# A decode step on one core: ScalarE sums 48 of a tile's 256 positions, and the maxima move into the next multiplication

## The chip, the cores and the metric

The kernel runs on one core of one Trainium2 chip. The metric is the device time of one launch in microseconds, taken over several runs. One of the runs was recorded by the hardware profiler; every time below that belongs to an instruction comes from that execution, counted from its span's start.

## The reference, cut to what matters

Two sequences of one new token each (B = 2, D = 512) go through attention over a cache of 8192 positions with 32 heads of 128, and then through a gated layer. All tensors are bfloat16.

```python
h  = x + attention(layernorm(x), k_cache, v_cache, wq, wo)
h2 = h + mlp(layernorm(h), W_gate, W_up, W_down)

# attention, Sq = 1, 32 heads, Dh = 128, Sk = 8192
q      = x @ wq                                   # (2, 32, 1, 128)
scores = einsum("bhqd,bhkd->bhqk", q, k) * Dh ** -0.5
o      = einsum("bhqk,bhkd->bhqd", softmax(scores), v)
out    = o.reshape(2, 1, 4096) @ wo
# mlp: ((x @ W_gate) * (gate > 0) * (x @ W_up)) @ W_down, F = 1376
```

The two caches hold 268 MB together, the weights some 12.6 MB. Each element of the cache is used once.

## The kernel before, in words

**Tiles and steps.** There are 16 steps: for each of the two sequences, eight groups of four heads. A step works on a K tile and a V tile of 8.4 MB each: 128 partitions, 32 to a head, with 256 positions of 128 values in each partition. The tiles pass through three buffers, `buf[0..2]`. `k_at` and `v_at` say which: V(i) goes into the buffer of K(i) once K(i) has been used up (except V(0) and V(15)), and K(i+1) into the buffer of V(i-2). All loads are issued on the SP queue, in the order K(i+1), V(i), and each waits for its buffer to be free. The projection weights `wq` and the row of queries `qrow` lie in `buf[1]` at the start, where V(0) goes; the output and MLP weights go into the buffer of K(15) at the end.

**Scores of step i** (`scores(i)`). VectorE multiplies the whole K tile in place by the query, spread over the partitions in `qrep` (line 344). Then it halves the 128 values of a position by additions, 128 to 64 to 32 to 16 to 8 (line 373), and a reduction sums the last eight into a column of `scol` (line 377). The last `NACT[i]` positions are left out of this tree: ScalarE sums each by a copy with `accum_out` (line 362), 8 positions in most steps, 24 and 32 in the first two, 16 in the last. Then VectorE takes the maximum of `scol` in each partition (`pm`, line 385), and TensorE spreads it with the softmax scale (`mx_ps`, line 387).

**The step before, in between.** After the multiplication of step i come `collect(i-2)` (ScalarE copies the finished products out of PSUM, line 434), `powers(i-1)` (VectorE reduces `mx_ps` to the negated maximum `nm`, line 303; ScalarE computes the exponentials into `pgz` in four instructions, line 306), `turn(i-2)` (TensorE turns collected products into columns) and `values(i-1)` (TensorE multiplies V(i-1) by the powers, 64 products in a loop, line 422; for the last two steps 256 small products, line 408). The order of the instructions on TensorE, VectorE, ScalarE and the SP queue is the order of the program.

**The ends.** Before step 0 the queries are made in eight groups (`make_q`): four products into `q_ps`, a copy by ScalarE into `qrow`, eight small products that spread them into `r_ps`, and a copy into `qrep`. In step 15, 48 of the positions are not multiplied by VectorE: TensorE transposes them eight at a time (line 326), ScalarE copies the transposed block into `kT` (line 331), and TensorE multiplies it by the query (line 335). After step 15 come the weights' loads (lines 464 to 482), `powers(15)`, `values(15)`, the output projection (line 516) and the MLP (lines 552 to 598).

Of the kernel before, what the change touches and what calls it, by code (L numbers as in the profile page):

```python
# [7 lines left out]
ACT = mybir.ActivationFunctionType  # L8
# [15 lines left out]
def kernel(  # L24
# [13 lines left out]
    nc = tc.nc  # L38
# [14 lines left out]
    TPC = 8  # L53
    NPE = 48
    T4 = 4
# [56 lines left out]

    qrep = consts.tile([P, B, NG, Dh], bf16)
    pgz = consts.tile([P, NT * H4], bf16)
# [54 lines left out]
    with tc.manual_schedule(engines=ORDERED):  # L169
# [62 lines left out]


        def make_q(n):
            q_ps = ps2.tile([P, 512], f32, tag="tp")
# [5 lines left out]
            nc.scalar.activation(out=qrow[0:B, n * 512:(n + 1) * 512], in_=q_ps[0:B, :], func=ACT.Copy)  # L241
            r_ps = ps2.tile([P, B, Dh], f32, tag="tp", name="r_ps")
# [52 lines left out]


        mx = {}

        def powers(i):
            b, g = steps[i]  # L300
            mx_ps, scol = mx.pop(i)
            nm = small.tile([P, H4], f32, tag="nm")
            nc.vector.tensor_reduce(out=nm, in_=mx_ps, axis=AXIS.X, op=ALU.min)  # L303
            for j in range(H4):
# [6 lines left out]
        def scores(i):  # L311
            b, g = steps[i]
            kt = buf[k_at[i]]
            npe = NPE if i == N - 1 else 0
            nmul = NT - npe
            nv = nmul - NACT[i]
            scol = small.tile([P, NT], f32, tag="scol")

            if npe:
                sc_ps = ps.tile([P, NPE, H4], f32, tag="sc")  # L320

                def transposed(c0):
                    t_ps = ps2.tile([P, TPC, P], bf16, tag="tp", name="t_ps")
                    for k in range(TPC):
                        t = nmul + c0 + k
                        nc.tensor.transpose(t_ps[:, k, :], kt[:, t * Dh:(t + 1) * Dh], ident)  # L326
                    return t_ps

                t_ps = transposed(0)
                for c0 in range(0, NPE, TPC):  # L330
                    nc.scalar.activation(out=kT, in_=t_ps.rearrange("p t s -> p (t s)"), func=ACT.Copy)  # L331
                    if c0 + TPC < NPE:
                        t_ps = transposed(c0 + TPC)
                    for t in range(TPC):
                        nc.tensor.matmul(  # L335
                            out=sc_ps[:, c0 + t, :], lhsT=kT[:, t * P:(t + 1) * P], rhs=_free(qT, b, [[B, H4]]),
                            start=True, stop=True,
                        )

            pieces = 4 if i == 0 else 1  # L340
            for t0 in range(0, NT, NT // pieces):
                n = min(NT // pieces, nmul - t0)
                kv = _free(kt, t0 * Dh, [[Dh, n], [1, Dh]])
                nc.vector.tensor_tensor(  # L344
                    out=kv, in0=kv, in1=_free(qrep, (b * NG + g) * Dh, [[0, n], [1, Dh]]), op=ALU.mult,
                )

            if i >= 2:
                collect(i - 2)
            if i >= 1:  # L350
                powers(i - 1)
            if i >= 2:
                turn(i - 2)
            left = waiting[:]
            if i >= 1:
                values(i - 1)
                tc.no_sync_barrier()
                if i + 1 < N:
                    load_k(i + 1)
            for t in range(nv, nmul):  # L360
                whole = small.tile([P, Dh], f32, tag="whole")
                nc.scalar.activation(  # L362
                    out=whole, in_=kt[:, t * Dh:(t + 1) * Dh], func=ACT.Copy, accum_out=scol[:, t:t + 1],
                )
            if npe:
                for j in range(H4):
                    r = slice(j * QP, (j + 1) * QP)
                    nc.scalar.activation(out=scol[r, nmul:NT], in_=sc_ps[r, :, j], func=ACT.Copy)
            width = Dh
            while width > 8:  # L370
                half = width // 2
                lo = _free(kt, 0, [[Dh, nv], [1, half]])
                nc.vector.tensor_tensor(  # L373
                    out=lo, in0=lo, in1=_free(kt, half, [[Dh, nv], [1, half]]), op=ALU.add,
                )
                width = half
            nc.vector.tensor_reduce(  # L377
                out=scol[:, 0:nv], in_=_free(kt, 0, [[Dh, nv], [1, 8]]), axis=AXIS.X, op=ALU.add,
            )

            for e in left:
                waiting.remove(e)
                normalise(e)
# [3 lines left out]
            nc.tensor.matmul(  # L387
                out=mx_ps.rearrange("p a b -> p (a b)"), lhsT=_free(pm, 0, [[0, P]]), rhs=nscale,
                start=True, stop=True,
            )  # L390
            mx[i] = mx_ps, scol

# [89 lines left out]
        nc.sync.dma_start(out=wd_r[0:LASTW], in_=_dram(B_W_down, FULL * P * D, [[D, LASTW], [1, D]]))  # L482

        turn(N - 2)
        powers(N - 1)
# [142 lines left out]
```

## Time and profile before

| | us |
|---|---|
| runs (3) | 675.11, 675.25, 677.73; median 675.25 |
| profiled execution, its own time | 676.83 |
| its span | 675.0 |
| PE busy | 365.0 (54%) |
| VectorE (DVE) busy | 573.7 (85%) |
| ScalarE (ACT) busy | 151.9 (23%) |
| bytes moved | 281.29 MB, mean 417 GB/s over the span |

How to read it: PE is TensorE, DVE is VectorE, ACT is ScalarE, SP the queue that issues the loads. A row of a timeline has start, duration, engine, line, operation, what it writes and reads, and in brackets how long its engine had been idle and for what it waited. A row of the groups has a count, the busy time, the mean of one in nanoseconds, and the idle time before. A row of the windows has the stretch, its length, the busy time of each engine, TensorE's granted clock, the DMA engines' busy share and the rate in GB/s.

### The profile page before, as it was taken

The numbers are of one execution on the slowest core, as the hardware profiler recorded it, in microseconds if no ns is written. First come the engines' busy times: TensorE is split into PE (matmuls) and PEld (weight loads), VectorE is DVE, ScalarE is ACT, GpSimd is POOL, SyncE is SP. The second block draws the span as 40 slices with busy tenths as digits, with TensorE's granted clock in tenths as the row PEclk, the third lists the DMA queues.
The fourth block names the chain that finished last, engine by engine and source line by source line (L and its number), as shares of the span: only waits on it lengthen the run. The fifth ranks groups of instructions, "written<-read, shape, count | busy, mean of one in ns | idle before, by whom it ended". The sixth has DMA issues, their size and how long they took to land. (4 is left out here: it accounts for less than half of the span.)

```text
span 675.0 us, 7725 instructions
## 1 busy us (share of the span) xinstructions
PE 365.0 (54%) x1963; PEld 126.5 (19%) x1963; DVE 573.7 (85%) x164; ACT 151.9 (23%) x525; POOL 8.5 (1%) x52
## 2 busy tenths in 40 slices
PE   2710373736647373663727466274745737277666
PEld 1100011111111121111102111011211111012556
DVE  0899989699897989979797997989899797998801
ACT  2360634003030401303030030303103040221820
POOL 5000000000000000000000000000000000000000
PEclk9999997987959698796969869598896959789555
DMA  9999999999999999999999999999999999999996
GB/s 371 438 433 435 435 373 435 435 435 435 377 436 435 435 427 435 435 377 431 431 432 419 396 435 416 435 400 435 424 416 435 396 435 404 431 416 412 417 417 255
DMA packets 6918, 281.29 MB, mean 417 GB/s; under 512 B 786, under 2 KB 884, under 8 KB 1524
## 3 DMA queue, kind: packets, MB, share of 16 engines
q1 hardware_dynamic: 6896, 281.06, 98.0%
q8 instruction: 10, 0.16, 0.1%
q14 instruction: 8, 0.07, 0.0%
q10 hardware_dynamic: 4, 0.00, 0.0%
HBM read 281.05 MB, written 0.00 MB: 416 GB/s over the span
## 5 line engine op out<-in xcount | busy, mean ns | idle before, releaser
L422 PE MATMUL po<-buf,pgz 128*16 x868 | 288.9, 410 | 90.0 <-issue 88.3
L344 DVE TENSOR_TENSOR buf<-buf,qrep 128x32768 bf16<-128x32768 bf16 (+2 forms) x19 | 272.9, 14362 | 52.4 <-DMA buf<-in_A_k_cache_dram 52.4
L373 DVE TENSOR_TENSOR buf<-buf 128x15872 bf16<-128x15872 bf16 (+7 forms) x64 | 252.0, 3937 | 1.7
L422 PEld LDWEIGHTS po<-buf,pgz 128*16 x868 | 78.8, 91 | 305.6 <-issue 264.2
L396 PE MATMUL po<-buf,pgz 128*16 128x512 bf16 x28 | 14.3, 614 | 158.5 <-ACT whole L362 158.5
L434 ACT ACTIVATE ob<-po 16x512 f32<-16x512 f32 x14 | 8.2, 585 | 325.0 <-PEq L416 324.9
L306 ACT ACTIVATE pgz<-scol,nm 32x256 bf16<-32x256 f32 x64 | 55.1, 862 | 111.0 <-DVE nm L303 106.2
L362 ACT ACTIVATE whole<-buf 128x128 f32<-128x128 bf16 x176 | 54.4, 309 | 6.0 <-DVE buf L344 0.5
L377 DVE TENSOR_REDUCE scol<-buf 128x248 f32<-128x1984 bf16 (+3 forms) x16 | 34.7, 2170 | 1.6
L362 ACT ACTIVATION_READ_ACCUMULATOR whole<-buf 128x1 f32 x176 | 32.8, 186 | 0.0
L396 PEld LDWEIGHTS po<-buf,pgz 128*16 128x16 bf16 x28 | 1.4, 90 | 160.9 <-issue 160.9
L387 PE MATMUL mx_ps<-nscale,pm 128*128 128x128 f32 x32 | 8.0, 334 | 24.9 <-DVE pm L385 19.8
L237 PE MATMUL q_ps<-buf,xn 128*2 128x512 bf16 x32 | 14.9, 621 | 2.9 <-DMA buf<-in_A_wq_dram 2.9
L408 PE MATMUL o_ps<-pgz,buf 128*128 128x4 bf16 x512 | 14.2, 166 | 3.4 <-issue 3.4
L306 ACT ACTIVATION_READ_ACCUMULATOR pgz<-scol,nm 32x1 f32 x64 | 16.0, 250 | 0.0
L293 DVE RECIPROCAL rz<-o_ps 128x4 f32<-128x4 f32 (+2 forms) x4 | 1.0, 253 | 17.3 <-PE o_ps L408 17.3
L408 PEld LDWEIGHTS <-buf 128*128 128x128 bf16 x512 | 14.3, 105 | 3.5 <-issue 3.5
L331 ACT ACTIVATE kT<-t_ps 128x1024 bf16<-128x1024 bf16 x6 | 6.1, 1023 | 28.9 <-PE t_ps L326 26.4
L387 PEld LDWEIGHTS mx_ps<-nscale,pm 128*128 128x128 f32 x32 | 5.2, 202 | 29.1 <-issue 18.9
L385 DVE TENSOR_REDUCE pm<-scol 128x1 f32<-128x256 f32 x16 | 6.7, 418 | 2.1 <-ACT whole L362 0.8
L218 DVE COPY xc<-x_ps 128x8 f32<-128x8 f32 x1 | 0.2, 166 | 8.5 <-PE x_ps L214 8.5
L241 ACT ACTIVATE buf<-q_ps 2x512 bf16<-2x512 f32 x8 | 4.7, 586 | 11.2 <-PE q_ps L237 11.2
(89 smaller groups left out, 85.9 us busy)
## 6 DMA issues: line engine op xcount, KB each, us to landing
buf<-in_A_k_cache_dram SPq DMA_DIRECT2D x4, 2048.0 KB, 23.7
buf<-in_A_v_cache_dram SPq DMA_DIRECT2D x2, 4096.0 KB, 24.8
buf<-in_A_wq_dram SPq DMA_DIRECT2D x1, 4096.0 KB, 12.6
buf<-in_A_wo_dram SPq DMA_DIRECT2D x1, 2048.0 KB, 17.3
buf<-in_A_wo_dram SPq DMA_DIRECT2D x2, 1024.0 KB, 20.2
buf<-in_B_W_gate_dram SPq DMA_DIRECT2D x1, 1376.0 KB
buf<-in_B_W_up_dram SPq DMA_DIRECT2D x1, 1376.0 KB, 25.8
buf<-in_B_W_down_dram SPq DMA_DIRECT2D x1, 768.0 KB, 26.9
```

The source lines that it names most:

```text
L237: nc.tensor.matmul(out=q_ps[0:B, :], lhsT=xn[:, c, :], rhs=wq_sb[:, c, n * 512:(n + 1) * 512], start=(c == 0), stop=(c == KC - 1),)
L306: nc.scalar.activation(out=_free(pgz[r, :], j, [[H4, NT]]), in_=scol[r, :], func=ACT.Exp, scale=SCALE, bias=nm[r, j:j + 1], accum_out=zc[r ...
L344: nc.vector.tensor_tensor(out=kv, in0=kv, in1=_free(qrep, (b * NG + g) * Dh, [[0, n], [1, Dh]]), op=ALU.mult,)
L362: nc.scalar.activation(out=whole, in_=kt[:, t * Dh:(t + 1) * Dh], func=ACT.Copy, accum_out=scol[:, t:t + 1],)
L373: nc.vector.tensor_tensor(out=lo, in0=lo, in1=_free(kt, half, [[Dh, nv], [1, half]]), op=ALU.add,)
L377: nc.vector.tensor_reduce(out=scol[:, 0:nv], in_=_free(kt, 0, [[Dh, nv], [1, 8]]), axis=AXIS.X, op=ALU.add,)
L385: nc.vector.tensor_reduce(out=pm, in_=scol, axis=AXIS.X, op=ALU.max)
L387: nc.tensor.matmul(out=mx_ps.rearrange("p a b -> p (a b)"), lhsT=_free(pm, 0, [[0, P]]), rhs=nscale, start=True, stop=True,)
L396: nc.tensor.matmul(out=made[i][0:H4 * T4, :], lhsT=pgz[:, u * H4 * T4:(u + 1) * H4 * T4], rhs=v[:, u * T4 * Dh:(u + 1) * T4 * Dh], start=( ...
L408: nc.tensor.matmul(out=o_of(i)[:, 0, H4 * g:H4 * (g + 1)], lhsT=v[:, t * Dh:(t + 1) * Dh], rhs=pgz[:, H4 * t:H4 * (t + 1)], start=(t == 0) ...
L422: nc.tensor.matmul(out=made[i][0:H4 * T4, :], lhsT=pgz[:, bass.ds((w * LOOP + u) * (H4 * T4), H4 * T4)], rhs=v[:, bass.ds((w * LOOP + u) * ...
L434: nc.scalar.activation(out=ob[32 * k:32 * k + H4 * T4, :], in_=made.pop(i)[0:H4 * T4, :], func=ACT.Copy,)
```

## The change

- `NACT` becomes 48 for most steps, 64 for step 1 and 32 for step 15. These are now the first positions of the tile, not the last.
- The multiplication is in three parts: the positions that ScalarE sums, then 144 (`MIDDLE`), then the rest. In step 0 it stays in four pieces.
- The maximum of step i-1 and its product on TensorE move out of step i-1 into step i, between the first and the second part (`best(i - 1)`). `powers(i-1)` comes after the second part. `scol` now has two buffers.
- ScalarE sums 16 positions (`FIRST`) before `collect` and `powers`, the others after `values`. Its full-width output, which nobody reads, goes to PSUM (`whole` from pool `ps`, tag `acc`) instead of SBUF.
- The projections run one group ahead: `make_q(n)` now comes before `spread_q(n - 1)`. `qrep` becomes one tile for each sequence, so the copy into it is two instructions; `kT` uses the room of the first one.
- Step 15: 32 positions instead of 48 go through TensorE; their first two blocks are transposed after the second part of the multiplication, the copies into `kT` come after `powers(14)`, and `values(14)` after them. The maximum of step 15 is taken after the weights' loads in the program.

```diff
-    NPE = 48
+    NPE = 32
+    FIRST = 16
+    MIDDLE = 144
...
-    qrep = consts.tile([P, B, NG, Dh], bf16)
+    qrep = [consts.tile([P, NG, Dh], bf16, name=f"qrep{b}") for b in range(B)]
...
-    kT = consts.tile([P, TPC * P], bf16)
+    kT = qrep[0].rearrange("p g d -> p (g d)")
...
-    NACT = {i: (24, 32)[i] if i < 2 else 16 if i == N - 1 else 8 for i in range(N)}
+    NACT = {i: 64 if i == 1 else 32 if i == N - 1 else 48 for i in range(N)}
...
-            nc.scalar.activation(out=qrep[:, :, n, :], in_=r_ps, func=ACT.Copy)
+            for b in range(B):
+                nc.scalar.activation(out=qrep[b][:, n, :], in_=r_ps[:, b], func=ACT.Copy)
...
-        for n in range(NG):
+        make_q(0)
+        spread_q(0)
+        make_q(1)
+        for n in range(2, NG):
             make_q(n)
+            spread_q(n - 1)
+        spread_q(NG - 1)
...
+        def best(i):
+            pm = small.tile([P, 1], f32, tag="pm")
+            nc.vector.tensor_reduce(out=pm, in_=scols[i], axis=AXIS.X, op=ALU.max)
+            mx[i] = ps.tile([P, H4, QP], f32, tag="mx", name="mx_ps")
+            nc.tensor.matmul(
+                out=mx[i].rearrange("p a b -> p (a b)"), lhsT=_free(pm, 0, [[0, P]]), rhs=nscale,
+                start=True, stop=True,
+            )
...
+            def mult(t0, t1):
+                kv = _free(kt, t0 * Dh, [[Dh, t1 - t0], [1, Dh]])
                 nc.vector.tensor_tensor(
-                    out=kv, in0=kv, in1=_free(qrep, (b * NG + g) * Dh, [[0, n], [1, Dh]]), op=ALU.mult,
+                    out=kv, in0=kv, in1=_free(qrep[b], g * Dh, [[0, t1 - t0], [1, Dh]]), op=ALU.mult,
                 )
-            if i >= 2:
-                collect(i - 2)
-            if i >= 1:
+            def sum_up(t0, t1):
+                for t in range(t0, t1):
+                    whole = ps.tile([P, Dh], f32, tag="acc", name="whole")
+                    nc.scalar.activation(
+                        out=whole, in_=kt[:, t * Dh:(t + 1) * Dh], func=ACT.Copy, accum_out=scol[:, t:t + 1],
+                    )
...
+            if i == 0:
+                for t0 in range(0, NT, NT // 4):
+                    mult(t0, t0 + NT // 4)
+                sum_up(0, na)
+            else:
+                mult(0, na)
+                best(i - 1)
+                mult(na, na + MIDDLE)
+                if last:
+                    t_ps = [transposed(c0) for c0 in (0, TPC)]
+                sum_up(0, FIRST)
+                if i >= 2:
+                    collect(i - 2)
                 powers(i - 1)
-            if i >= 2:
-                turn(i - 2)
-            left = waiting[:]
-            if i >= 1:
+                if i >= 2:
+                    turn(i - 2)
+                left = waiting[:]
+                if last:
+                    mult(na + MIDDLE, nmul)
+                    for e in left:
+                        waiting.remove(e)
+                        normalise(e)
...
+                    for c0 in range(0, NPE, TPC):
+                        nc.scalar.activation(out=kT, in_=t_ps.pop(0).rearrange("p t s -> p (t s)"), func=ACT.Copy)
+                        if c0 + 2 * TPC < NPE:
+                            t_ps.append(transposed(c0 + 2 * TPC))
...
                 values(i - 1)
                 tc.no_sync_barrier()
-                if i + 1 < N:
+                if not last:
                     load_k(i + 1)
-            for t in range(nv, nmul):
...
+                    mult(na + MIDDLE, nmul)
+                sum_up(FIRST, na)
+            n = nmul - na
             width = Dh
             while width > 8:
                 half = width // 2
-                lo = _free(kt, 0, [[Dh, nv], [1, half]])
+                lo = _free(kt, na * Dh, [[Dh, n], [1, half]])
...
-            pm = small.tile([P, 1], f32, tag="pm")
-            nc.vector.tensor_reduce(out=pm, in_=scol, axis=AXIS.X, op=ALU.max)
-            mx_ps = ps.tile([P, H4, QP], f32, tag="mx")
...
+        best(N - 1)
         turn(N - 2)
         powers(N - 1)
```

More of the change, by code (lines that the diff above doesn't have):

```diff
@@ L312, in scores @@
             b, g = steps[i]
+            last = i == N - 1
             kt = buf[k_at[i]]
[L314 to L343, printed above, removed]
+            nmul = NT - (NPE if last else 0)
+            na = NACT[i]
+            scol = scols[i] = small.tile([P, NT], f32, tag=f"scol{i % 2}", name="scol")
+            def mult(t0, t1):
+                kv = _free(kt, t0 * Dh, [[Dh, t1 - t0], [1, Dh]])
                 nc.vector.tensor_tensor(
-                    out=kv, in0=kv, in1=_free(qrep, (b * NG + g) * Dh, [[0, n], [1, Dh]]), op=ALU.mult,
+                    out=kv, in0=kv, in1=_free(qrep[b], g * Dh, [[0, t1 - t0], [1, Dh]]), op=ALU.mult,
@@ L377, in scores @@
             nc.vector.tensor_reduce(
-                out=scol[:, 0:nv], in_=_free(kt, 0, [[Dh, nv], [1, 8]]), axis=AXIS.X, op=ALU.add,
+                out=scol[:, na:nmul], in_=_free(kt, na * Dh, [[Dh, n], [1, 8]]), axis=AXIS.X, op=ALU.add,
             )
-            for e in left:
-                waiting.remove(e)
-                normalise(e)
-            pm = small.tile([P, 1], f32, tag="pm")
-            nc.vector.tensor_reduce(out=pm, in_=scol, axis=AXIS.X, op=ALU.max)
-            mx_ps = ps.tile([P, H4, QP], f32, tag="mx")
[L387 to L391, printed above, removed]
+            if i and not last:
+                for e in left:
+                    waiting.remove(e)
+                    normalise(e)
         def products(i, u0, u1):
```

35 lines of the change are left out of this document (23 added, 12 removed).

## The prediction

> **What bounds the kernel now.** I read the page first: its head, its slices and the DMA line.
>
> ```profile
> span 675.0 us, 7725 instructions
> PE 365.0 (54%) x1963; PEld 126.5 (19%) x1963; DVE 573.7 (85%) x164; ACT 151.9 (23%) x525; POOL 8.5 (1%) x52
> GB/s 371 438 433 435 435 373 435 435 435 435 377 436 435 435 427 435 435 377 431 431 432 419 396 435 416 435 400 435 424 416 435 396 435 404 431 416 412 417 417 255
> DMA packets 6918, 281.29 MB, mean 417 GB/s; under 512 B 786, under 2 KB 884, under 8 KB 1524
> ```
>
> VectorE is busy 85% of the span, but the second thing to see is the rate: 417 GB/s over the whole span, and 435 in the better slices. The cache is streamed through three buffers, and the transfers never really stop. So the question is not which engine is busiest but what holds the transfers from 435 in the other slices. Next come the timelines of the SP queue, which issues the loads, and of VectorE, whose big multiplication starts when a K tile has landed.
>
> ```profile
> 54.87 0.33 SPq L144 DMA_DIRECT2D buf<-in_A_k_cache_dram  x1
> 90.19 0.33 SPq L144 DMA_DIRECT2D buf<-in_A_v_cache_dram  x1
> 128.21 0.33 SPq L144 DMA_DIRECT2D buf<-in_A_v_cache_dram  x1
> 142.80 0.33 SPq L144 DMA_DIRECT2D buf<-in_A_k_cache_dram  x1
> 169.54 0.33 SPq L144 DMA_DIRECT2D buf<-in_A_v_cache_dram  x1
> 406.38 0.33 SPq L144 DMA_DIRECT2D buf<-in_A_v_cache_dram  x1
> 638.56 2.31 SPq L464 DMA_DIRECT2D buf<-in_A_wo_dram  x3
> 655.91 0.34 SPq L482 DMA_DIRECT2D buf<-in_B_W_down_dram  x1
> ```
>
> ```profile
> 32.98 4.43 DVE L344 TENSOR_TENSOR buf<-buf,qrep 128x8192 bf16<-128x8192 bf16 x1 [0.47 <-DMA buf<-in_A_k_cache_dram]
> 55.24 17.21 DVE L344 TENSOR_TENSOR buf<-buf,qrep 128x32768 bf16<-128x32768 bf16 x1
> 92.26 17.22 DVE L344 TENSOR_TENSOR buf<-buf,qrep 128x32768 bf16<-128x32768 bf16 x1 [1.65 <-DMA buf<-in_A_k_cache_dram]
> 133.58 17.23 DVE L344 TENSOR_TENSOR buf<-buf,qrep 128x32768 bf16<-128x32768 bf16 x1 [4.91 <-DMA buf<-in_A_k_cache_dram]
> 150.72 0.28 DVE L303 TENSOR_REDUCE nm<-mx_ps 128x4 f32<-128x128 f32 x1
> 150.93 16.22 DVE L373 TENSOR_TENSOR buf<-buf 128x15872 bf16<-128x15872 bf16 x4
> 167.25 2.22 DVE L377 TENSOR_REDUCE scol<-buf 128x248 f32<-128x1984 bf16 x1
> 172.20 17.23 DVE L344 TENSOR_TENSOR buf<-buf,qrep 128x32768 bf16<-128x32768 bf16 x1 [2.21 <-DMA buf<-in_A_k_cache_dram]
> 411.13 17.23 DVE L344 TENSOR_TENSOR buf<-buf,qrep 128x32768 bf16<-128x32768 bf16 x1 [4.00 <-DMA buf<-in_A_k_cache_dram]
> 450.31 17.23 DVE L344 TENSOR_TENSOR buf<-buf,qrep 128x32768 bf16<-128x32768 bf16 x1 [2.77 <-DMA buf<-in_A_k_cache_dram]
> 609.81 14.03 DVE L344 TENSOR_TENSOR buf<-buf,qrep 128x26624 bf16<-128x26624 bf16 x1 [3.27 <-DMA buf<-in_A_k_cache_dram]
> 623.95 12.73 DVE L373 TENSOR_TENSOR buf<-buf 128x12288 bf16<-128x12288 bf16 x4
> 636.78 1.75 DVE L377 TENSOR_REDUCE scol<-buf 128x192 f32<-128x1536 bf16 x1
> ```
>
> Call K(i) and V(i) the tiles of step i; V(i) goes into the buffer of K(i), so it is issued when VectorE and ScalarE have read K(i) for the last time. K(3) lands at 133.58 and K(15) at 609.81: twelve steps in 476.23 us, 39.69 us each. VectorE needs 167.25 + 2.22 - 133.58 = 35.9 us of a step and V(i) follows at once (169.54). What is left, the lead of V(i)'s issue over K(i+1)'s landing, is small: 5.37 us for V(2) (128.21 against 133.58), 2.66 for V(3) (169.54, 172.20), 4.75 for V(9) (406.38, 411.13). The step after each: 172.20 - 133.58 = 38.62 us behind the lead of 5.37, and 450.31 - 411.13 = 39.18 us behind 4.75. The eleven steps after the first average (609.81 - 172.20)/11 = 39.78. The windows show where the difference lies.
>
> ```profile
> 128.00:134.00 6.00, 4.19 (x14) 1.11 (x13) 0.98 (x3) 0.00 (x0) 0.00 (x0) 1.00 1.22 524
> 168.00:174.00 6.00, 4.33 (x15) 1.19 (x14) 3.69 (x3) 0.00 (x0) 0.00 (x0) 1.00 0.88 339
> 287.00:293.00 6.00, 4.38 (x14) 1.19 (x14) 2.35 (x3) 0.00 (x0) 0.00 (x0) 1.00 0.86 306
> ```
>
> Last column: GB/s, counted where packets start. Around the change from K(3) to V(2), issued early, there is no dip; around that from K(4) to V(3), and a like one three steps on, 339 and 306. So a V load issued under about five microseconds ahead finds some DMA engines already dry. About a microsecond a step is lost there, and the bound of a step is the release of K(i) by VectorE, 35.9 us after landing.
>
> **The change part by part.** *The steady step.* ScalarE sums 48 positions instead of 8, so the halving tree has 208 positions, not 248. Rows: 248 positions cost 16.22 + 2.22 = 18.44 us, 192 cost 12.73 + 1.75 = 14.48; 0.0707 us a position, so 208 cost 15.6, a saving of 2.8 us. The multiplication is cut in three: 17.2 us as before and two more starts, put at 0.1 us each (the 8192 and 32768 forms, 4.43 and 17.23, leave 0.16 for a start). The maximum of the step before (0.42) moves from after the tree to after the first third; before, it stood behind V's release, now it is ahead of it. So VectorE releases K(i) at 17.2 + 0.2 + 0.4 + 0.3 + 15.6 = 33.7 us after landing, 2.2 earlier than 35.9.
>
> ScalarE must be done as well. Its rows:
>
> ```profile
> 37.45 0.31 ACT L362 ACTIVATE whole<-buf 128x128 f32<-128x128 bf16 x1 [0.48 <-DVE buf L344]
> 37.88 0.31 ACT L362 ACTIVATE whole<-buf 128x128 f32<-128x128 bf16 x1
> 229.72 0.87 ACT L306 ACTIVATE pgz<-scol,nm 32x256 bf16<-32x256 f32 x1 [6.87 <-DVE nm L303]
> 232.98 0.25 ACT L306 ACTIVATION_READ_ACCUMULATOR pgz<-scol,nm 32x1 f32 x1
> L434 ACT ACTIVATE ob<-po 16x512 f32<-16x512 f32 x14 | 8.2, 585 | 325.0 <-PEq L416 324.9
> L331 ACT ACTIVATE kT<-t_ps 128x1024 bf16<-128x1024 bf16 x6 | 6.1, 1023 | 28.9 <-PE t_ps L326 26.4 <-PE sc_ps L335 2.6
> ```
>
> A sum starts every 0.43 us, and the four exponentials of a step take 232.98 + 0.25 - 229.72 = 3.5. The change sends the sum's unused output to PSUM, which no row of before does. The nearest rows are reads from PSUM: 585 ns for 512 elements and 1023 for 1024 leave 0.15 fixed, against 0.20 for the SBUF-to-SBUF sum (0.31 less 128 at the same 0.85 ns). So a sum costs from 0.36, should both halves of the pair gain, up to 0.43, should nothing change, or more if writing to PSUM is slow there; I take 0.40. The order on ScalarE: 16 sums (from 3.3 us, the first third's end, to 9.7), the copy of the products (0.6), then the exponentials, which need the minimum VectorE takes behind the middle third: 3.3 + 0.4 + 144 x 0.0673 (17.23/256) + 0.3 = 13.7. They end at 17.3, and 32 sums end at 30.1 with 0.40, at 31.1 with 0.43. Both lie before 33.7: the added 40 sums are hidden, and at 0.51 us a sum the cover is gone. The Trainium skill says that ScalarE reaches PSUM faster than SBUF (ScalarE: Activation LUTs, "Step-by-step: what each stage is for"). By that rule the sum at the end of this part would be nearer the lower end of the first two tiles' range, -2 us further; no run here shows it yet.
>
> Two more waits move. TensorE's product of the maximum now stands before turn and values of the same step, as in the old order, behind the values of two steps before; those end where the next K is issued, at 142.80, 9.2 us after K(3) landed. VectorE reads the result at 13.4, so 4 us cover it. The exponentials come 4 us earlier than before (they started 229.72, behind a whole multiplication), but V(i-1) lands only about 19.3 us after K(i) (half of 38.62), so TensorE's values start near 20, hardly sooner, and the K issues behind them have 10 us in hand as before.
>
> Now the lead: step less 33.7. The mean step of 39.78 has a lead of 39.78 - 35.9 = 3.9, and a lead of 5.37 gave 38.62: a microsecond of lead is worth 0.8 us. A step P with lead P - 33.7 then solves P = 38.62 + 0.8 x (5.37 - P + 33.7), P = 38.8. Since V(9) with 4.75 still lost 0.5, I take 38.9, bounds 38.62 and 39.4. Twelve steps: 12 x (38.9 - 39.69) = -9.5 us, from -12.8 to -3.5.
>
> *The first two tiles.* The new order of the q projections is hidden: the first multiplication pieces wait for DMA up to 32.98, and V(0), issued behind the projections, lands behind K(1) anyway; cover gone, it would cost its queue time behind 55. ScalarE's sums of tile 0 start at 37.45 now, behind the last piece; they are now the first positions, landed long before, and wait only for the projections' copies on ScalarE, which I put at 36. So 48 sums end at 55.2. VectorE: pieces end 37.4, tree 53.0, first 64 positions of tile 1 57.3, maximum 57.7, 144 positions 67.4, minimum 67.7; exponentials to 71.4; then 48 sums of tile 1, 19.2 us at 0.40: V(1) issued at 90.6, against 90.19 now. VectorE alone would be done at 67.7 + 3.2 + 14.5 = 85.4, so here ScalarE is the bound. At 0.36 it is 88.7, at 0.43 92.2. K(2) landed at 92.26, so V(1) is late either way and its delay counts in full: +0.5 us, from -1.5 to +2. K(2), issued at 55.2 rather than 54.87, is behind V(0) and costs nothing.
>
> *The last step.* 32 positions instead of 48 go over TensorE, ScalarE sums 32 instead of 16, the kT copies wait for the exponentials, and the multiplication covers 224 positions, not 208: 14.03 + 16 x 0.0673 = 15.1 us. Before, the chain of work that ended last ran here:
>
> ```profile
> 633.85 0.59 PE o_ps L285 x2
> 643.32 0.32 DVE rz L293
> 645.44 0.87 ACT pgz L306 x2
> 649.61 5.01 PE o_ps L408 x188
> 672.48 0.18 DVE y L598
> ```
>
> and the DMA issues say of the last weights (size, then microseconds from issue to landing):
>
> ```profile
> buf<-in_B_W_down_dram SPq DMA_DIRECT2D x1, 96.0 KB, 14.9
> ```
>
> Counted from K(15)'s landing at 609.81: exponentials at 35.6, values of V(15) at 39.8, the last cast at 62.7. New: VectorE 15.1 + 0.4 + 0.3 + 0.6 (two instructions for a division, 0.3 each by the row of 643.32) + 0.2 + 14.5 (192 positions) = 31.1, against 28.7 now (638.56, where the weights are issued); ScalarE: exponentials to 16.4, four kT copies of 1.02, with TensorE's products between some 1.5 a round, to 22.5, four small copies at 0.2, 16 sums to 29.8. So the weights are issued 2.4 us later, but V(15) is in transfer until about 38.6, which covers it by 7 us. TensorE's values(14) starts behind the kT products near 22.7 and needs 9 us, as now (633.85 to 643.32), to about 32; the maximum of step 15 no longer waits behind the division that follows it, so the exponentials run from 32.8 instead of 35.6. The chain of work comes 2.8 us earlier, but the transfers do not: the last weights were issued at 655.91 and landed 14.9 later, 61.0 after K(15). K(15)'s followers are 16.8 MB of V and 8.4 MB of weights, 3 x 19.3 = 57.9 us and a landing; they can gain what V(14)'s late issue costs (about 1 us). So -1.5 us, from -2.5 to 0.
>
> **The sum.** -9.5 + 0.5 - 1.5 = -10.5 us. The profiled execution took 676.83 us (span 675.0 and 1.8 around it), so it would take 666.3. The median of the runs is 675.25, 1.58 lower; the same difference off the median gives 664.8, my forecast. About 0.5%, 3.4 us, is what a measurement of this kernel can tell from no change.
>
> **The rivals.**
>
> *The loss at the K-to-V change is not the late issue.* The dips could be the DMA engines' own drift: the rate in the slices falls from 435 to about 415 in the later half while leads hardly change, and V(9) with 4.75 still lost half a microsecond. Then steps stay near 39.6 and only the ends move: 12 x 0.1 + 1 - 0.5 = 1.7 less, 673.5 us. Against it: the one early V was followed by the shortest step and showed no dip. Chance 0.14, with everything in between that leaves less than 3.4 us.
>
> *ScalarE becomes the bound, and the kernel is slower.* One mechanism: a sum whose output goes to PSUM takes longer, not shorter. At 0.60 us the steady release is 17.3 + 32 x 0.6 = 36.5, no better than 35.9, so the steps gain nothing; and tile 0's sums end at 64.8, delay tile 1's maximum by 7 us, and V(1) goes out near 107 instead of 90.19, with the transfers idle meanwhile: 675.25 + 17 - 1.5 = 691 us. It decides from about 0.52 us a sum, where V(1) at 100 eats the gain. For it: the 48 sums of tile 1 already are the bound of that tile. Against: PSUM reads are cheaper, not dearer. The Trainium skill (ScalarE: Activation LUTs, "Rules for kernel authors") tells one to keep add and mul on VectorE, which is faster an element. The rows agree on the price, 0.43 us a position against 0.0707, and this kernel can pay it only because ScalarE is idle 77% of the span. Chance 0.08.
>
> *The lead saturates fully.* With 38.62 a step, -1 for the first two tiles and -2.5 at the end the time is 675.25 - 12.8 - 3.5 = 659. This is the far end of my own case.
>
> **How the numbers follow.** Forecast case (steps of 38.62 to 39.3) 0.78: 664.8 is its likeliest. No gain or next to none 0.14, of which half still lies over 0.5% faster. ScalarE bound 0.08. Faster 0.85, within 0.5% 0.07, slower 0.08. The range: low end with 38.7 a step (-11.9) and -1.8 for the two ends together, 661.5; high end 672.5, reaching the start of the no-gain case; about 0.1 lies above it and 0.1 below.
>
> **What would show it.** In the timelines of the changed kernel: V loads issued 33 to 34 us after K lands and over five ahead of the next K; K landings 38.6 to 39.2 apart; no window near 300 GB/s at the K-to-V changes; the sums 0.36 to 0.43 apart; VectorE's idle time before its first multiplication 4 to 5 us a step. V(1) issued between 88 and 93. Wrong it would be if sums are over 0.5 apart, if VectorE waits for a maximum on TensorE in the middle of its multiplications, or if leads of five microseconds come with steps of 39.6.

## The result, and the profile after

The changed kernel took 672.31 us (median of 6 runs, 671.97 to 673.3), the kernel before in the same session 675.62 (6 runs, 675.11 to 677.73): a ratio of 0.9949, 95% interval 0.9933 to 0.9964. It is faster by half a per cent, and the forecast was 664.8, over three times that gain. The profiled execution took 671.97 us, 4.86 less than before's 676.83. Cut at the landings of K(3) and K(15), as the forecast was:

| stretch | before | after | change | forecast |
|---|---|---|---|---|
| start to K(3) | 133.58 | 134.35 | +0.77 | +0.5 |
| twelve steps, K(3) to K(15) | 476.23 (39.69 each) | 471.57 (39.30 each) | -4.66 | -9.5 |
| K(15) to the end | 67.02 | 66.05 | -0.97 | -1.5 |

Of the 5.6 us that the forecast promised and the chip did not give, 4.8 are missing in the steady steps. The head of the page after:

```profile
span 670.3 us, 8852 instructions
PE 358.5 (53%) x1931; PEld 124.0 (18%) x1931; DVE 536.1 (80%) x194; ACT 388.5 (58%) x1715; POOL 8.5 (1%) x52
GB/s 371 443 436 438 435 321 439 438 438 435 435 427 407 426 438 435 438 434 435 430 435 422 411 435 418 438 399 438 435 435 434 415 427 415 431 430 426 415 411 225
DMA packets 6928, 281.37 MB, mean 420 GB/s; under 512 B 786, under 2 KB 884, under 8 KB 1524
```

VectorE has 38 us less to do, ScalarE 237 us more in 1190 more instructions, and the rate went from 417 to 420 GB/s only. Apart from the last slice, one is worse than any of before: 321. The SP queue's timeline and VectorE's:

```profile
92.63 0.33 SPq L147 DMA_DIRECT2D buf<-in_A_v_cache_dram  x1
125.77 0.33 SPq L147 DMA_DIRECT2D buf<-in_A_v_cache_dram  x1
167.99 0.33 SPq L147 DMA_DIRECT2D buf<-in_A_v_cache_dram  x1
637.57 1.28 SPq L491 DMA_DIRECT2D buf<-in_A_wo_dram  x3
```

```profile
134.35 3.36 DVE L344 TENSOR_TENSOR buf<-buf,qrep 128x6144 bf16<-128x6144 bf16 x1 [8.65 <-DMA buf<-in_A_k_cache_dram]
166.04 1.89 DVE L412 TENSOR_REDUCE scol<-buf 128x208 f32<-128x1664 bf16 x1
173.72 3.36 DVE L344 TENSOR_TENSOR buf<-buf,qrep 128x6144 bf16<-128x6144 bf16 x1 [5.79 <-DMA buf<-in_A_k_cache_dram]
213.11 3.36 DVE L344 TENSOR_TENSOR buf<-buf,qrep 128x6144 bf16<-128x6144 bf16 x1 [5.82 <-DMA buf<-in_A_k_cache_dram]
251.81 3.36 DVE L344 TENSOR_TENSOR buf<-buf,qrep 128x6144 bf16<-128x6144 bf16 x1 [5.12 <-DMA buf<-in_A_k_cache_dram]
291.19 3.36 DVE L344 TENSOR_TENSOR buf<-buf,qrep 128x6144 bf16<-128x6144 bf16 x1 [5.81 <-DMA buf<-in_A_k_cache_dram]
605.92 2.29 DVE L344 TENSOR_TENSOR buf<-buf,qrep 128x4096 bf16<-128x4096 bf16 x1 [5.83 <-DMA buf<-in_A_k_cache_dram]
```

V(3) goes out at 167.99, 33.64 us after K(3) landed (forecast 33.7), and 5.73 us ahead of K(4) at 173.72. VectorE then waits 5.8 us for it. The lead is 5.06 to 5.94 us in eleven of the twelve steady steps and 4.48 in the other. But the steps are 39.37, 39.39, 38.70 and 39.38 us long: one of these four is the 38.7 that the forecast had at the low end of its range, the others stand 0.68 above it. The windows, and beneath them the row of before for the first (same stretch of 88 to 94):

```profile
88.00:94.00 6.00, 4.48 (x14) 1.16 (x14) 1.86 (x1) 4.29 (x22) 0.00 (x0) 1.00 0.45 153
168.00:174.00 6.00, 4.21 (x15) 1.17 (x14) 0.28 (x1) 0.00 (x0) 0.00 (x0) 1.00 0.86 371
287.00:293.00 6.00, 4.33 (x14) 1.14 (x14) 1.81 (x1) 0.00 (x0) 0.00 (x0) 1.00 1.01 415
```

```profile
88.00:94.00 6.00, 4.20 (x14) 1.11 (x13) 3.58 (x3) 2.01 (x10) 0.00 (x0) 1.00 0.58 197
```

In the steady steps the dip at the change from K to V is shallower (339 before, 371 now; 306, now 415). At 88 to 94 it is deeper: V(1), issued at 92.63 instead of 90.19, is later than K(2)'s landing.

What tells the short step from its neighbours is in the DMA queues, asked for over one step each: first the step 213.11 to 251.81 (38.70 us), then 251.81 to 291.19 (39.38 us).

```profile
q1 hardware_dynamic: 287, 16.71, 99.7%
```

```profile
q1 hardware_dynamic: 291, 16.97, 100.4%
q14 instruction: 1, 0.01, 0.1%
```

The long step has a packet of 8 KB on queue 14, which loads instructions; the short one has none. Over the whole span the page of after, and that of before, say of this queue (packets, MB, share):

```profile
q14 instruction: 18, 0.15, 0.1%
```

```profile
q14 instruction: 8, 0.07, 0.0%
```

Ten packets more for 1190 more ScalarE instructions, one for each 119. In the twelve steady steps of after, the ten with such a packet took 39.36 to 39.58 us and the two without 38.70 and 38.73. The trace's records of single packets show how 8 KB of 16.8 MB can cost 0.68 us: each of the 16 DMA engines carries eight packets of 64 KB of a tile, 2.42 us each, one behind the other, and closes the tile with a short record of 4 bytes; VectorE starts some 0.4 us behind the last of these. (The trace does not name a packet's engine; two packets are put on one engine here where the second starts as the first ends.) The instruction packet at 261.00 took 0.32 us on one engine, and the cache packet that followed on it took 2.80 us instead of 2.42: together 0.70. This engine closes the tile last of the sixteen, at 290.71 against a median of 288.10, and VectorE starts at 291.19. Followed so, the engine with a packet of queue 14 is the last of the sixteen in all ten steps that have one, and from 204.69 on it seems to be one and the same engine, so that the delays add up on it (at three places two packets fit the chain equally well).

### The profile page after: what moved, and what is told of

Same layout as the page of the kernel before. It is cut to its first block, busy times and chain, and to the rows that moved or that the text cites. A ratio compares the mean times of both kernels' runs of the same rounds, so it can differ in the third digit from the quotient of the medians.

```text
span 670.3 us, 8852 instructions
## 1 busy us (share of the span) xinstructions
PE 358.5 (53%) x1931; PEld 124.0 (18%) x1931; DVE 536.1 (80%) x194; ACT 388.5 (58%) x1715; POOL 8.5 (1%) x52
## 5 line engine op out<-in xcount | busy, mean ns | idle before, releaser
L344 DVE TENSOR_TENSOR buf<-buf,qrep 128x8192 bf16<-128x8192 bf16 (+3 forms) x49 | 278.4, 5681 | 89.7 <-DMA buf<-in_A_k_cache_dram 89.7
L351 ACT ACTIVATE whole<-buf 128x128 f32<-128x128 bf16 x768 | 216.0, 281 | 186.4 <-DVE buf L344 159.8
L408 DVE TENSOR_TENSOR buf<-buf 128x13312 bf16<-128x13312 bf16 (+3 forms) x64 | 216.1, 3377 | 2.2
L351 ACT ACTIVATION_READ_ACCUMULATOR whole<-buf 128x1 f32 x768 | 143.2, 187 | 0.2
L412 DVE TENSOR_REDUCE scol<-buf 128x208 f32<-128x1664 bf16 (+1 forms) x16 | 29.9, 1869 | 0.5
L242 PE MATMUL q_ps<-buf,xn 128*2 128x512 bf16 x32 | 11.1, 492 | 5.2 <-DMA buf<-in_A_wq_dram 3.0
## 6 DMA issues: line engine op xcount, KB each, us to landing
buf<-in_A_k_cache_dram SPq DMA_DIRECT2D x4, 2048.0 KB, 23.8
buf<-in_A_wo_dram SPq DMA_DIRECT2D x2, 1024.0 KB, 16.8
```

What stands on the lines that cost most here:

```text
L242: nc.tensor.matmul(out=q_ps[0:B, :], lhsT=xn[:, c, :], rhs=wq_sb[:, c, n * 512:(n + 1) * 512], start=(c == 0), stop=(c == KC - 1),)
L344: nc.vector.tensor_tensor(out=kv, in0=kv, in1=_free(qrep[b], g * Dh, [[0, t1 - t0], [1, Dh]]), op=ALU.mult,)
L351: nc.scalar.activation(out=whole, in_=kt[:, t * Dh:(t + 1) * Dh], func=ACT.Copy, accum_out=scol[:, t:t + 1],)
L408: nc.vector.tensor_tensor(out=lo, in0=lo, in1=_free(kt, na * Dh + half, [[Dh, n], [1, half]]), op=ALU.add,)
L412: nc.vector.tensor_reduce(out=scol[:, na:nmul], in_=_free(kt, na * Dh, [[Dh, n], [1, 8]]), axis=AXIS.X, op=ALU.add,)
```

## The experiments

The theory: each load of ScalarE's instructions delays a tile's landing by some 0.7 us, and the change brings one into nearly every step (**instruction loads**, mostly A in the expectations, each of which spells out its letters). Rivals: V still goes out too late (B); the loss is the stream's own pace or drift, whatever ScalarE loads (C, near the prediction's first rival); ScalarE's busy time or its traffic slows the transfers, not its instructions (**busy time**, D). For the first tiles: V(1) waits for ScalarE's sums of tiles 0 and 1, 48 and 64, and a sum takes 0.43 us because it waits for the one before it, which writes the same tile (E) or because it always takes that long (F). Ratios are to the kernel before, run beside each.

**tile1_48: 48 sums in step 1 instead of 64.**

```diff
-    NACT = {i: 64 if i == 1 else 32 if i == N - 1 else 48 for i in range(N)}
+    NACT = {i: 32 if i == N - 1 else 48 for i in range(N)}
```

> The changed kernel with 48 instead of 64 positions of tile 1 summed by ScalarE. Theory A (the first two tiles are ScalarE-bound: exponentials, then 48 sums of 0.434 us): after the exponentials only 32 sums are left, ScalarE is done near 85, VectorE near 87, V(1) is issued near 87 instead of 92.63, the gap in front of it (the transfers' rate falls to 321 GB/s in that slice) closes, and the kernel is 3.5 to 4.5 us faster than the changed one, about 668. Rival (the gap at 90 us has another cause, or is made up for later by a longer lead): within 1 us of the changed kernel.

669.85 us (668.06 to 672.01), ratio 0.9913 (0.9893 to 0.9933). From its SP queue and VectorE:

```profile
87.78 0.33 SPq L147 DMA_DIRECT2D buf<-in_A_v_cache_dram  x1
```

```profile
131.14 3.36 DVE L344 TENSOR_TENSOR buf<-buf,qrep 128x6144 bf16<-128x6144 bf16 x1 [5.55 <-DMA buf<-in_A_k_cache_dram]
```

V(1) goes out 4.9 us earlier and K(3) lands 3.2 earlier (131.14 against 134.35); the steps stay at 39.34. By the profiled executions it is 3.9 us faster than after, by the medians 2.5. What the late V(1) cost came from ScalarE's share of tile 1.

**dummy64: 64 one-column copies on ScalarE behind the sums of each step from 2 to 14.**

```diff
             sum_up(FIRST, na)
+            if 2 <= i < N - 1:
+                for _ in range(64):
+                    nc.scalar.activation(out=warm, in_=eps_col, func=ACT.Copy)
```

> The changed kernel with 64 one-column copies on ScalarE added behind the sums of each step from 2 to 14, where ScalarE has some 8 us of idle time and nothing waits for it. Theory A (instruction packets: every 128 instructions of ScalarE are fetched by an 8 KB packet on queue 14, all on one of the 16 DMA engines; each sets that engine, and with it the landing of the tile, back by 0.68 us): 832 instructions are 6 to 7 packets more, 24 to 25 on queue 14 instead of 18, and the kernel is 3.5 to 4.7 us slower, about 676; steps take 38.7, 39.4 or 40.1 by the number of packets in them. Rival B (the loss left in a step is a V load issued too late) and rival C (39.3 us is the stream's own pace): no change within 0.5 us, since V's release does not move.

678.93 us, ratio 1.0044 (1.003 to 1.0059): 6.6 us slower than after, more than expected. Two successive K landings, and the DMA queues between them:

```profile
252.97 3.36 DVE L344 TENSOR_TENSOR buf<-buf,qrep 128x6144 bf16<-128x6144 bf16 x1 [5.78 <-DMA buf<-in_A_k_cache_dram]
293.18 3.36 DVE L344 TENSOR_TENSOR buf<-buf,qrep 128x6144 bf16<-128x6144 bf16 x1 [6.63 <-DMA buf<-in_A_k_cache_dram]
```

```profile
q14 instruction: 2, 0.02, 0.1%
```

V(3) still goes out 33.64 us after K(3) and the transferred data are the same; yet this step of two packets lasts 40.21 us, and the twelve average 39.74. The copies also occupied ScalarE for some 15 us a step (one started every 0.23), so this run alone does not part instructions from busy time. `busy14`, with 14 copies of 1024 columns in place of the 64 small ones, was meant to part them and gave no time; `skip32_busy` below asks the same.

**share8: 8 sums a step, as before the change, with all the rest of the change.**

```diff
-    NACT = {i: 64 if i == 1 else 32 if i == N - 1 else 48 for i in range(N)}
+    NACT = {i: 64 if i == 1 else 32 if i == N - 1 else 48 if i == 0 else 8 for i in range(N)}
...
-                sum_up(0, FIRST)
+                sum_up(0, min(FIRST, na))
...
-                sum_up(FIRST, na)
+                sum_up(min(FIRST, na), na)
```

> The changed kernel with ScalarE's share set back to 8 positions in steps 2 to 14; order, maxima, projections and last step stay. VectorE's tree has 248 positions again, its release of K comes 2.8 us later, 36.5 us after landing, with the maximum now ahead of it. Theory A (instruction packets): some 8 packets fewer on queue 14, but V late again: steps of 39.7 to 40.1, 4 to 9 us slower than the changed kernel, 677 to 681. Rival C (39.3 is the stream's own pace and the release of K does not matter): within 1 us of the changed kernel.

678.87 us, ratio 1.0048 (1.0027 to 1.0069).

```profile
134.29 0.69 DVE L344 TENSOR_TENSOR buf<-buf,qrep 128x1024 bf16<-128x1024 bf16 x1 [5.35 <-DMA buf<-in_A_k_cache_dram]
611.78 2.29 DVE L344 TENSOR_TENSOR buf<-buf,qrep 128x4096 bf16<-128x4096 bf16 x1 [3.32 <-DMA buf<-in_A_k_cache_dram]
```

K(3) lands at 134.29 and K(15) at 611.78, 39.79 a step, with leads of 2.2 to 5 us: before's 39.69 again. The new order by itself brings the steps nothing, and with V(1) as late as in after the whole is slower. The gain of the change is the 40 positions more on ScalarE.

**sbuf_out: the sums' output in SBUF again, all else as after.**

```diff
-                    whole = ps.tile([P, Dh], f32, tag="acc", name="whole")
+                    whole = small.tile([P, Dh], f32, tag="whole", name="whole")
```

> The changed kernel with the unused output of the sums in SBUF, as before the change. Theory A (the interval between sums is set by the pair of instructions, not by where the output goes): an ACTIVATE of 309 instead of 281 ns, sums still every 0.43 us, time within 0.5 us of the changed kernel. Rival (the PSUM output hides part of the price, the sums would come at 0.46 or more from SBUF): V(1) 1 to 2 us later, the kernel 1 to 2 us slower.

673.29 us, ratio 0.9962 (0.9946 to 0.9977), overlapping that of after. The groups of ScalarE's instructions, of after and of this kernel (busy us, mean ns):

```profile
L351 ACT ACTIVATE whole<-buf 128x128 f32<-128x128 bf16 x768 | 216.0, 281 | 186.4 <-DVE buf L344 159.8 <-issue 3.0
```

```profile
L351 ACT ACTIVATE whole<-buf 128x128 f32<-128x128 bf16 x768 | 237.5, 309 | 190.1 <-DVE buf L344 164.0 <-issue 2.5
```

PSUM shortens the instruction from 309 to 281 ns, but in both kernels one sum starts every 0.43 us. The instruction's own time is not what spaces them.

**skip32: 32 of the 48 sums left out in steps 2 to 14, their columns set to zero by GpSimd.** VectorE's work and the V release stay as they are.

```diff
-            sum_up(FIRST, na)
+            if last or i == 1:
+                sum_up(FIRST, na)
...
+            if 2 <= i < N - 1:
+                nc.gpsimd.memset(scol[:, FIRST:na], 0.0)
```

> The changed kernel with the last 32 of ScalarE's 48 sums left out in steps 2 to 14 (their columns of the scores are set to zero by GpSimd instead); VectorE's work, and with it the release of K, stays as it is. This is the lead of the changed kernel without two thirds of ScalarE's instructions. Theory A (instruction packets on one DMA engine): 64 instructions fewer a step, 6 to 7 packets fewer on queue 14; steps of 38.7 where no packet falls and 39.4 where one does, mean about 38.95, and the kernel 3.5 to 5 us faster than the changed one, about 668. Rivals B (V loads still late) and C (39.3 is the stream's own pace): steps stay at 39.3, time within 1 us of the changed kernel.

667.14 us (666.82 to 667.89), ratio 0.9886 (0.9867 to 0.9906). Its K landings and the page's line on queue 14:

```profile
290.06 3.36 DVE L347 TENSOR_TENSOR buf<-buf,qrep 128x6144 bf16<-128x6144 bf16 x1 [5.12 <-DMA buf<-in_A_k_cache_dram]
328.75 3.36 DVE L347 TENSOR_TENSOR buf<-buf,qrep 128x6144 bf16<-128x6144 bf16 x1 [5.11 <-DMA buf<-in_A_k_cache_dram]
601.39 2.29 DVE L347 TENSOR_TENSOR buf<-buf,qrep 128x4096 bf16<-128x4096 bf16 x1 [5.80 <-DMA buf<-in_A_k_cache_dram]
```

```profile
q14 instruction: 11, 0.09, 0.0%
```

Step after step of 38.69 us, and an average of (601.39 - 133.99)/12 = 38.95: the forecast's 38.9. So the forecast's step was there to be had at this lead, and a drift that would hold whatever ScalarE loads is refuted. What took it away came with the 32 sums.

**skip32_busy: skip32, and 17 copies of 768 columns in each of these steps instead of the sums.**

```diff
+    spare = consts.tile([P, 768], bf16, name="spare")
...
+            else:
+                for _ in range(17):
+                    nc.scalar.activation(out=spare, in_=pgz[:, 0:768], func=ACT.Copy)
```

> The kernel that leaves out 32 of the 48 sums in steps 2 to 14, with 17 copies of 768 columns on ScalarE in their place: about as much ScalarE time as the sums left out (some 14 us a step), with 17 instructions instead of 64. Theory A (instruction packets): 221 instructions, one or two packets more than without the copies, 0.7 to 1.4 us slower than that kernel, 668.5; steps without a packet stay at 38.7. Rival D (ScalarE's busy time is what costs, not the number of its instructions): back at the changed kernel's 672.3.

668.46 us (668.17 to 670.14), ratio 0.9909 (0.989 to 0.9928). ScalarE is busy 406.4 us, more than in after (388.5) and against 221.2 in skip32, with 1104 instructions against 1715 and 883.

```profile
252.31 3.36 DVE L348 TENSOR_TENSOR buf<-buf,qrep 128x6144 bf16<-128x6144 bf16 x1 [5.12 <-DMA buf<-in_A_k_cache_dram]
291.01 3.36 DVE L348 TENSOR_TENSOR buf<-buf,qrep 128x6144 bf16<-128x6144 bf16 x1 [5.13 <-DMA buf<-in_A_k_cache_dram]
```

```profile
q14 instruction: 13, 0.11, 0.0%
```

The steps average 38.98 us, and eight of the twelve are under 39.0, as in skip32. Busy time as the cause falls; the number of instructions stands. Over the kernels whose V goes out 33.6 us after K:

| kernel | ScalarE instructions | q14 packets in the span | steady steps under 39.0 us, of 12 |
|---|---|---|---|
| dummy64 | 2547 | 24 | 0 |
| after, sbuf_out, inplace (below) | 1715 | 18 | 2 |
| tile1_48 | 1683 | 17 | 2 |
| skip32_busy | 1104 | 13 | 8 |
| skip32 | 883 | 11 | 8 |

Not each packet costs its 0.7 us: skip32, skip32_busy and tile1_48 have a step or two of 38.7 to 39.0 with a packet in it, before's first step (38.62) has one, and after's step of 38.73 has one of 16 KB on queue 8. For two of these the single packets say why: in skip32's step of 38.70 with a packet (at 259.53) the packet's engine closes the tile at 289.25 and another one last, at 289.59; in before's first step the packet's engine closes at 169.98 and the last at 171.84. A delay on an engine that is not the last costs the tile nothing. For the others the reason stays open.

**loop4_t48: the last 32 sums of a step in a hardware loop of eight rounds of four, to load fewer instructions (with 48 sums in step 1).**

> The changed kernel with 48 instead of 64 positions of tile 1, and with the last 32 sums of steps 2 to 14 written as a loop of eight rounds of four on ScalarE (the unused output goes back into K, in place). The instructions of a step fall from about 106 to 66 static ones. Theory A (instruction packets): 4 to 5 packets fewer, steps near 39.05, 3 us faster than the same kernel unrolled (669.85), about 667, if the loop's sums still come every 0.45 us or faster and its branches fetch nothing. Rival: the loop's branches fetch their targets again, or VectorE's tree waits for the in-place sums; then V's release moves later and the kernel is slower than unrolled, 672 or more.

1167.99 us, ratio 1.7308. The loop stands in a section of its own that ScalarE enters only after a wait, and VectorE's tree waits for it in turn, as the groups show:

```profile
L417 DVE TENSOR_TENSOR buf<-buf 128x13312 bf16<-128x13312 bf16 (+3 forms) x64 | 217.1, 3393 | 573.1 <-ACTq L403 571.3
```

The edit failed, and it says nothing on instruction loads. But inside the loop, where each sum wrote into its own place, one started every 0.29 us.

**inplace: each sum writes over the products that it read.**

```diff
-                    whole = ps.tile([P, Dh], f32, tag="acc", name="whole")
+                    whole = kt[:, t * Dh:(t + 1) * Dh]
                     nc.scalar.activation(
-                        out=whole, in_=kt[:, t * Dh:(t + 1) * Dh], func=ACT.Copy, accum_out=scol[:, t:t + 1],
+                        out=whole, in_=whole, func=ACT.Copy, accum_out=scol[:, t:t + 1],
```

> The changed kernel with the sums' unused output written back over the K positions themselves, so that no two sums write the same place; nothing else. Theory E (a sum waits for the end of the sum before it because both write the one tile whole): sums every 0.29 to 0.31 us, as in the loop seen before, instead of 0.43; ScalarE's 48 sums of tile 1 end near 86, with VectorE, instead of 92.6, the gap in front of V(1) closes and the kernel is 3 to 4 us faster than the changed one, about 668.5; the steady steps stay at 39.3, since their instruction packets stay. Rival F (the interval is the pair's own, whatever it writes): sums every 0.43 us, time within 0.5 us of the changed kernel.

669.45 us (668.12 to 670.02), ratio 0.9919 (0.9901 to 0.9936). ScalarE's timeline of after, then of this kernel:

```profile
90.04 0.28 ACT L351 ACTIVATE whole<-buf 128x128 f32<-128x128 bf16 x1
90.25 0.19 ACT L351 ACTIVATION_READ_ACCUMULATOR whole<-buf 128x1 f32 x1
90.47 0.28 ACT L351 ACTIVATE whole<-buf 128x128 f32<-128x128 bf16 x1
```

```profile
79.56 0.29 ACT L351 ACTIVATE buf<-buf 128x128 bf16<-128x128 bf16 x1
79.76 0.19 ACT L351 ACTIVATION_READ_ACCUMULATOR buf<-buf 128x1 f32 x1
79.85 0.29 ACT L351 ACTIVATE buf<-buf 128x128 bf16<-128x128 bf16 x1
```

With one shared output the next sum starts only when the read of the accumulator has ended (90.25 + 0.19, 90.47); with an output of its own it starts 0.09 us behind that read's start. All 64 sums of tile 1 stay on ScalarE, and V(1) goes out at 86.78 instead of 92.63; K(3) lands at 131.01. The steps, with after's 18 packets of queue 14, stay at 39.32. The edit also makes the output bf16 and puts it in SBUF. sbuf_out rules out the place; no run changes the type alone. The exponentials of the same trace write bf16 too and still start only when the read before them has ended (226.12 after 225.85 + 0.25), so the type alone does not bring the overlap. But the first sum behind them waits as well (227.01 after 226.73 + 0.25), though it writes elsewhere. That the sharing spaces the sums is likely, not shown.

**share32_t48** (32 sums a step, 48 in the first two) and **inplace_32** (in place, 32 sums a step, 48 and 64 in the first two) take fewer instructions without leaving work out.

> The changed kernel with 32 instead of 48 positions on ScalarE in steps 2 to 14 and 48 instead of 64 in tile 1. Theory A (instruction packets against lead): 32 instructions fewer a step, 3 to 4 packets fewer, worth 2.4 us; V's release 1.1 us later, at 34.8 us, a lead of 4.4, worth -0 to -5 us by how much of the loss at the change from K to V comes back. Between 667.5 and 673, and the trace tells the two apart: steps without a packet at 38.7 if the lead is enough, at 39.3 or more if it is not. Rival B (only the lead counts): all steps longer by 0.5 us or more, 674 or more.

> The same with 32 instead of 48 positions on ScalarE in steps 2 to 14. Theory A and E together: V(1) near 86, and 3 to 4 packets fewer against a lead 1.1 us shorter, as the run with 32 and 48 positions showed: 667 to 669, the steps without a packet at 38.7 to 38.8.

share32_t48: 668.94 us (666.23 to 669.83), ratio 0.9901 (0.9879 to 0.9923). 14 packets; most steps 38.7 to 39.6, but one of 40.48 and one of 41.32, so that the mean is 39.39. The longest follows a V load with a lead of 2.13 us, which looks like the old loss; yet in inplace_32 a lead of 2.38 was followed by 39.39, so this step's cause stays open. inplace_32: 668.75 us (667.17 to 669.63), ratio 0.9906 (0.9887 to 0.9926), 15 packets, leads of 3.9 to 4.8 but for that one, and (601.60 - 131.04)/12 = 39.21 a step. These two, inplace and tile1_48 are the versions that beat both kernels while doing all the work; their intervals overlap, and which is best stays open.

## Why the prediction was right and wrong

**The mechanism was right.** V(i) goes out 33.64 us after K(i)'s landing, forecast 33.7; the lead is 5.7 us, forecast 5.2; ScalarE's 48 sums are hidden behind VectorE. That lead does bring a step of 38.7: skip32 shows it for eight steps of twelve. share8 shows the reverse: without the lead, 39.79.

**The step that failed is the steady step's P = 38.9,** 12 x (38.9 - 39.69) = -9.5. It measured 39.30, -4.66. The forecast priced the 40 added sums of a step by ScalarE's time and found them hidden, which they were. It did not count that these are 80 more instructions a step, as rows of ACTIVATE and of ACTIVATION_READ_ACCUMULATOR, which have to be loaded over the same DMA engines that bound the kernel. Before's page had the row that could have raised the question, 8 packets on queue 14 for 525 instructions, and the forecast did not read it. Ten of twelve steps took 0.7 us longer for it (39.41 on average against 38.71), 7 us in all, more than the 4.8 that were missing: the steps without a packet, 38.70, are better than the 38.9 forecast. The Trainium skill (Runtime: NRT & Kernel Launch, "Instruction fetch mechanics") says that each engine's sequencer fetches its instructions over a DMA queue of its own, 256 instructions to 16 KiB, and that the cost of a block's boundary is mostly hidden. The trace agrees on the queue and on the size of an instruction (8 KB for about 119 to 139 of them, from after and dummy64), but a packet of queue 14 is 8 KB, half of such a block. The load is mostly hidden from ScalarE here (3.0 us of idle time before its sums fall under issue in the whole span of after), but not from the tile that shares a DMA engine with it.

**The bound "39.4" was met by luck.** The forecast's upper bound on a step, put there for leads that pay less than hoped, is where the steps came out, for another reason; 672.31 lies inside the range (up to 672.5) for no better one. The first rival's 673.5 us lies 1.2 from the result, but its mechanism, a loss that the lead does not touch, is refuted by skip32. What a microsecond of lead is worth stays open: the forecast's 0.8 us came from before's leads, and by it a lead of 3.94 us would give a step of 39.8; inplace_32 had one of 38.79 behind that lead (V(2) at 127.10, K(3) at 131.04), with no packet in it.

**The first two tiles: the price of a sum.** Forecast +0.5 at 0.40 us a sum, with V(1) at 90.6, or 92.2 at 0.43. Measured: 0.43, V(1) at 92.63, K(3) +0.77. The choice of the middle between 0.36 and 0.43 was the error: the interval is not set by the memory that the output lies in, as sbuf_out shows, but by what inplace changed, most likely that all sums share one output. The rule taken from the Trainium skill (ScalarE: Activation LUTs, "Step-by-step: what each stage is for"), that ScalarE reaches PSUM faster, is borne out by 281 against 309 ns and changed nothing in the time. Here the change also gave time away: 64 sums in step 1 delay K(3) by 3.2 us against 48.

**The last step.** Forecast -1.5, measured -0.97. The weights go out 31.65 us after K(15) landed (637.57 - 605.92; forecast 31.1). VectorE's last maximum and TensorE's product of it:

```profile
637.58 0.42 DVE L315 TENSOR_REDUCE pm<-scol 128x1 f32<-128x256 f32 x1 [1.05 <-ACT whole L351]
```

```profile
639.70 0.65 PE mx_ps L317 x2
640.38 0.29 DVE nm L326
640.67 0.10 DVE rz L306
640.77 0.86 ACT pgz L329 x2
```

VectorE waits 1.05 us for ScalarE's last sum, and the product waits behind values(14), which ends at 639.70 (33.8 after K(15), forecast 32). The exponentials start at 34.85, forecast 32.8, before 35.6. The chain of work gained 0.75 us of the 2.8 that the forecast saw in it. Most of the difference is values(14): forecast from 22.7 with 9 us, it ran from 23.8 and took 10.0. Before's rows already had 9.5 (633.85 to 643.32), not 9, and the pause in the middle grew. The chain of before, then of after:

```profile
639.59 1.85 issue
```

```profile
630.14 6.00 PE o_ps L435 x225
636.14 2.58 issue
638.72 0.98 PE o_ps L435 x31
```

Beside each of the two pauses a packet of 16 KB of instructions goes over queue 8 (at 639.06 in before, 636.23 in after); that TensorE waits for it is not shown.

**The warnings.** That leads of five microseconds might come with steps of 39.6 was named as what would make the forecast wrong; they came with 39.4, and the cause was not the lead. A wait for the maximum on TensorE amid the multiplications was named as a sign of error. It stands in VectorE's timeline at 462.65, 0.52 us long; the lead of that step was 4.48 us, the shortest of the twelve:

```profile
462.65 0.29 DVE L326 TENSOR_REDUCE nm<-mx_ps 128x4 f32<-128x128 f32 x1 [0.52 <-PE mx_ps L317]
```

## What to carry to other kernels

In a kernel that is bound by its transfers, work on an idle engine need not be free once its own time is hidden: in this one its instructions were loaded over the same DMA engines, and a tile landed when the slowest of them was done. Count the added instructions against the instruction queue's packets in the profile before giving an idle engine many small ones. And before putting an unread output into a faster memory, look at whether the next instruction waits for that output: writing in place gave more (0.43 to 0.29 us) than PSUM did (nothing).

## What the runs showed of the hardware that was not expected

- An 8 KB instruction packet took 0.32 us on its DMA engine and lengthened the 64 KB packet behind it from 2.42 to 2.80 us. Most steps with one were 0.68 us longer than those without (39.38, 38.70), and in all ten such steps of after the engine that carried it closed the tile last.
- 128-element sums with one shared output start 0.43 us apart, in SBUF and in PSUM alike; written in place, in bf16 and with an output each, they start 0.29 us apart, though the instruction itself is no shorter (295 ns against 281).
- A one-column copy on ScalarE took 0.20 us and started every 0.23, not much less than a sum of 128 elements.
